# A gate in pairs of slices, fewer copies and a new instruction list in a linear-attention and expert-layer kernel

## The chip, the core and the metric

One core of a Trainium2 chip runs the whole program. The metric is device time in microseconds; for the kernel before it is the median of three runs. One further execution was taken by the hardware profiler, and all rows here are of that one.

## The reference, cut to what matters

```python
k_n = k / (norm(k) + 1e-6)
for t in range(S):                        # B, H, S, D = 4, 8, 768, 48
    y[t] = q[t] @ state
    state += beta[t] * outer(k_n[t], v[t] - k_n[t] @ state)
x = y as [3072 tokens, 384]
h = x @ w_in                              # w_in 384 x 2048
x = (h * clip(h + 3, 0, 6) / 6) @ w_out   # the dense layer, w_out 2048 x 384
# then eight experts (384 -> 1024 -> 384), each token to the one with the largest gate
```

## The kernel before

The program has two parts. The first part, which the change edits, works through the sequence in 12 chunks of 64 steps (32 rows of 4 batches times 8 heads, handled as two halves of 128 partitions, so 24 iterations `it`), and runs the first seven 128-wide slices of the dense layer's hidden width (NF1 = 7) for each chunk's 256 tokens as soon as these are known. The second part does the remaining nine slices on 512 tokens at a time, and then the experts.

The first part is written as some 30 Python generators (streams), each of which yields one engine instruction or a group. `drive` asks them in the order of the letters of ORDER, so ORDER alone sets the order in which instructions reach each engine; each engine then works its own queue in that order and waits where data are missing.

Names that recur. `kr`, `kn`, `Kbd` are the keys as loaded, normed, and split in two half-precision parts. `pG` is the product of keys with themselves, whose diagonal 32 x 32 blocks ScalarE copies to `Dt` (four copies an iteration, one for each 32 partitions); VectorE transposes `Dt` into `Bt` and solves a triangular system in `Xp` with `sub` as its scratch tile. `uH`/`uL`, `W`, `S`, `Spr` belong to the recurrence over chunks. `vsq`, `sums`, `tot`, `ptot`, `ssq`, `eiv`, `elv`, `sgv`, `sd` belong to a running sum of squares of v, from which each chunk's power-of-two scale is made: one round for each chunk. `xTH`/`xTL` are a chunk's transposed output in two parts.

`narrow_first` prepares a dense-layer weight: ScalarE takes the absolute value into `nws`, VectorE bounds it from below, and three more VectorE instructions move bits. It runs 14 times, twice for each of the seven slices.

The gate of the dense layer is in `m_stream`: for each slice nine matmuls into `ph`, 256 columns, then

```python
yield ACT.activation(t_, ph, ACTF.Relu, bias=half, scale=1.0 / 6.0)
yield DVE.scalar_tensor_tensor(t_, t_, 1.0, ph, ALU.min, ALU.mult)
yield ACT.activation(gH, t_, ACTF.Copy)
yield POOL.tensor_tensor(gL, t_, gH.bitcast(FP32), ALU.subtract)
```

and, one slice later, six matmuls of `gH`/`gL` with the second weight into `py`. `ph` has two halves of one bank used in turn, `t` one buffer of 256 columns, `gH` and `gL` two each.

In the rows nearly all of the first part has line L36, the helper that issues each instruction; the tiles tell them apart.

Of the kernel before, what the change touches and what calls it, by code (L numbers as in the profile page):

```python
# [71 lines left out]
def kernel(ctx: ExitStack, tc: tile.TileContext, q, k, v, beta, w_in, w_out, w_gate, w1, w2, out):  # L72
# [141 lines left out]
    with ExitStack() as ax:  # L214
# [136 lines left out]
        def scale_stream():  # L351

            last = None
            for s in range(NS):
                yield "next"
                yield from need(("V", s))
                sums = tmp([128, 2], FP32, "sums", 2)
                for bp in range(2):
                    yield ACT.activation(tmp([128, H, D], FP32, "vsq"), vrs[s][:, bp], ACTF.Square, accum_out=sums[:, bp:bp + 1])
                tot = tmp([128, 1], FP32, "tot", 2)  # L360
                if s:
                    yield DVE.scalar_tensor_tensor(tot, sums[:, 0:1], last, sums[:, 1:2], ALU.add, ALU.add)
                else:
                    yield DVE.tensor_tensor(tot, sums[:, 0:1], sums[:, 1:2], ALU.add)
# [10 lines left out]
                sgt[s] = dict(r=sd[:, 0:1], p=sd[:, 1:2], v=sg[:, 0], i=sg[:, 1])  # L375
                done.add(("sc", s))
# [24 lines left out]
        def n_stream():  # L401

            for g in range(NI // 4):
                yield "next"
                ss = tmp([128, 4, H], FP32, "ss")
                for j in range(4):
                    yield from need(("kl", 2 * g + j // 2))
                    sq_ = tmp([128, H, D], FP32, "ksq" if g or j % 2 else "vsq")
                    yield ACT.activation(sq_, ks[2 * g + j // 2][:, j % 2], ACTF.Square)
                    yield DVE.tensor_reduce(ss[:, j], sq_, AX.X, ALU.add)  # L410
# [418 lines left out]
        def narrow_first(src, n):  # L829
# [7 lines left out]
            yield DVE.tensor_scalar(bf, bf, 2.0 ** -15, None, ALU.max)  # L837
# [59 lines left out]
        nph = [0]  # L897
        yps = {}

        def m_stream():  # L900
            for s in range(NS):
# [3 lines left out]
                py = [clk.tile(psA, [128, 512], FP32, f"py{t}", 1, f"py{t}") for t in range(2)]  # L905
                pend = []
                for f in range(NF1 + SKM):
                    if f < NF1:
                        if not s:
                            yield from need(("wi", f))  # L910
                        fs = slice(f * 128, (f + 1) * 128)
                        ph = phb[:, nph[0] % 2]
                        nph[0] += 1
                        for c in range(KD):
                            yield [PE.matmul(ph, wi[a][:, c, fs], xt[x][:, c], start=c == 0 and n == 0, stop=c == KD - 1 and n == 2)
                                   for n, (a, x) in enumerate(((0, 0), (0, 1), (1, 0)))]
                        t_ = tmp([128, 256], FP32, "t", 1)
                        yield ACT.activation(t_, ph, ACTF.Relu, bias=half, scale=1.0 / 6.0)
                        yield DVE.scalar_tensor_tensor(t_, t_, 1.0, ph, ALU.min, ALU.mult)
                        gH, gL = tmp([128, 256], FP32R, "gH", SKM + 1), tmp([128, 256], FP32R, "gL", SKM + 1)  # L920
                        yield ACT.activation(gH, t_, ACTF.Copy)
                        yield POOL.tensor_tensor(gL, t_, gH.bitcast(FP32), ALU.subtract)
                        pend.append((f, gH, gL))
                    if f == NF1 - 1:
                        done.add(("Y", s))
                    if f >= SKM:
                        fp, gh, gl = pend.pop(0)
                        if not s:
                            yield from need(("wo", fp))
                        for t in range(2):  # L930
                            ts_ = slice(t * 128, (t + 1) * 128)
                            o = py[t][:, 0:YW]
                            yield [PE.matmul(o, gh[:, ts_], wo[0][:, fp], start=fp == 0, stop=False),
                                   PE.matmul(o, gh[:, ts_], wo[1][:, fp], start=False, stop=False),
                                   PE.matmul(o, gl[:, ts_], wo[0][:, fp], start=False, stop=fp == NF1 - 1)]
# [13 lines left out]
        def drive(streams):  # L949
# [33 lines left out]
            "kkkkkaaaakbrbbbbbsbrbbprbrpbsrbsjjrjbsrbbsqbjsnqrnqsnssqqqqqqsprnqnqnrqq1smrnronsr1mnprqrrsomsmnossn",  # L983
            "snnrssoqsmnnmmnsmsmmsrsqnrrnmosrnro0nsm0jqmmaarammmmmsqomqrsbjjsqbqrasmbmmbqmksommsmmsmkkmbrkms6rorm",
            "bmkkkmdmkmhrhssssshblrlslblqlespbrbrssslrklbrllelblblblbsblleplqsldslrlrlelnrnlnnnnllrllslelnlnnsnsl",
            "lrescslsnlqlsrrnlnllelnkllaslqessamllnrmqsrlrlmslrbmlrlmslscrnmlslmlqbnelenramsmasrqbsqscllbmlbllbll",
            "qlnsbllmmrbirnmkmmbibk7riqmsbemefmbsmserscqmqefsiifmii2sb3i3imsbs33ii2mm7misqmmibs116smfr220hf10h1h0",
            "1f0fesl11b0esnf0ls1ll0slll230ele4ln1e23n02dfni4nrq10ilf0lfinl0dililsin1isis0nirfgslg1e5li12fge5lecse",
            "al0lge0fsgnlsl0glm33tfa0lt1tltmqldnc11tts1l00ststt0t1ntelltlltmt0tllpn0pllqlqltetttnl1tmmmtfnttltml1",
            "4bl4qntttlbltmtqs1tm0nl1lltnbtsdttltttnm7qlllmstmfsqlc1mtl1lql8af8lmtntlt0ttttleq1tfltasmnmt0clfm1ll",  # L990
            "tmmmllelttttt0s1t0itttimeg50beq1ittqtbgmqb5gbmgqtgbbgbib3q22mbmmmqit7itit2tbmtqbt3ebitpp2titt080qtth",
            "ihfth0feb00ttlit0tt6tqtltlqil0itqn3f3nnllq0l2qltfld9t21llttldi4it1lini4l1tlqiqlttt0tn1tl3tc1t3ftl12e",
# [498 lines left out]
```

## Time and profile before

| | us |
|---|---|
| median of three runs (980.76 to 981.46) | 980.83 |
| profiled execution | 983.78 |
| its span, first to last instruction | 982.1 |
| TensorE busy in the span | 887.7 |
| VectorE | 584.1 |
| ScalarE | 571.4 |
| GpSimd | 429.9 |

The rows name engines as PE (TensorE), PEld (its weight loads), DVE (VectorE), ACT (ScalarE), POOL (GpSimd), SP (the queue that issues most DMAs). A group's row tells what is written from what, partitions by elements, the count, busy time, the mean of one in ns, and the idle time just before. TensorE's rows are pipelined, so that its busy time holds the tails of matmuls that overlap.

### The profile page before, as it was taken

The numbers are of one execution on the slowest core, as the hardware profiler recorded it, in microseconds if no ns is written. First come the engines' busy times: TensorE is split into PE (matmuls) and PEld (weight loads), VectorE is DVE, ScalarE is ACT, GpSimd is POOL, SyncE is SP. The second block draws the span as 40 slices with busy tenths as digits, with TensorE's granted clock in tenths as the row PEclk, the third lists the DMA queues.
The fourth block names the chain that finished last, engine by engine and source line by source line (L and its number), as shares of the span: only waits on it lengthen the run. The fifth ranks groups of instructions, "written<-read, shape, count | busy, mean of one in ns | idle before, by whom it ended". The sixth has DMA issues, their size and how long they took to land.

```text
span 982.1 us, 27912 instructions
## 1 busy us (share of the span) xinstructions
PE 887.7 (90%) x11582; PEld 822.5 (84%) x11582; DVE 584.1 (59%) x1612; ACT 571.4 (58%) x1201; POOL 429.9 (44%) x445
## 2 busy tenths in 40 slices
PE   2426999999989999999999999999999999999997
PEld 2425889889978888888788899899899999999996
DVE  8998998988879887564576455653553222121221
ACT  6858997897878967765556332333325453354521
POOL 5346555554535623333532113303105934765751
PEclk9999798999999999999989999999999999999999
DMA  7889998899697877356465233322208634533500
GB/s 148 149 159 151 170 178 150 157 158 167 149 165 149 176 168 172 92 160 218 142 200 162 99 105 116 107 65 98 91 29 289 219 98 131 176 119 116 174 21 21
DMA packets 250921, 137.85 MB, mean 140 GB/s; under 512 B 195427, under 2 KB 235685, under 8 KB 250784
## 3 DMA queue, kind: packets, MB, share of 16 engines
q1 hardware_dynamic: 242960, 117.77, 53.1%
q0 software_dynamic: 7280, 17.41, 5.4%
q8 instruction: 92, 1.51, 0.6%
q10 hardware_dynamic: 544, 0.80, 0.2%
q14 instruction: 45, 0.37, 0.1%
HBM read 71.56 MB, written 35.50 MB: 109 GB/s over the span
## 4 chain that ended last, share of the span: by engine, by line
PE 63%; DVE 18%; ACT 7%; issue 7%; POOL 3%; DMA 1%; SPq 0%; POOLq 0%; ACTq 0%; DVEq 0%
PE ph L1320 11%; PE ph L1111 9%; PE ph L36 6%; PE py L36 6%; PE py L1336 4%; PE py L1335 4%; PE py L1334 4%; PE pz L1099 3%; PE pz L1101 3%; PE pz L1100 3%; DVE Xp L36 3%; DVE sub L36 3%; PE pO L36 2%; DVE nws L36 2%; PE pW L36 2%
## 5 line engine op out<-in xcount | busy, mean ns | idle before, releaser
L1115 DVE SCALAR_TENSOR_TENSOR hL<-ph,hH 128x384 fp32r<-128x384 f32 (+6 forms) x64 | 36.1, 564 | 163.5 <-ACT hH L1114 163.5
L36 POOL TENSOR_TENSOR gL<-t,gH 128x256 fp32r<-128x256 f32 x84 | 64.8, 771 | 153.3 <-ACT gH L36 139.4
L1114 ACT ACTIVATE hH<-ph 128x384 fp32r<-128x384 f32 (+6 forms) x64 | 31.7, 495 | 105.1 <-PE ph L1111 105.1
L36 PE MATMUL ph<-xTH,wiH 128*128 128x256 f32 x252 | 76.4, 303 | 10.4 <-DVE t L36 9.5
L1323 ACT ACTIVATE t<-ph,half 128x512 f32<-128x512 f32 x54 | 37.2, 689 | 77.2 <-PE ph L1320 76.9
L1280 POOL DMA_INDIRECT slots<-row,di x24 | 23.9, 998 | 125.0 <-DVE di L1272 119.5
L1324 DVE SCALAR_TENSOR_TENSOR t<-t,ph 128x512 f32<-128x512 f32 x54 | 37.1, 687 | 65.6 <-ACT t L1323 65.4
L1099 PE MATMUL pz<-a2H,hH 128*128 128x384 f32 (+1 forms) x216 | 73.2, 339 | 0.4 <-ACT hH L1114 0.4
L1100 PE MATMUL pz<-a2L,hH 128*128 128x384 f32 (+1 forms) x216 | 72.4, 335 | 0.0
L1101 PE MATMUL pz<-a2H,hL 128*128 128x384 f32 (+1 forms) x216 | 72.4, 335 | 0.0
L1132 POOL DMA_INDIRECT out_dram<-yo,rw x29 | 28.1, 969 | 100.6 <-ACT yo L1131 96.3
L36 PE MATMUL ph<-xTL,wiH 128*128 128x256 f32 x252 | 71.1, 282 | 0.0
L36 PE MATMUL ph<-xTH,wiL 128*128 128x256 f32 x252 | 71.0, 282 | 0.0
L1328 DVE TENSOR_TENSOR gL<-t,gH 128x512 fp32r<-128x512 f32 x54 | 46.7, 865 | 32.7 <-ACT gH L1327 32.5
L36 DVE TENSOR_TENSOR Xp<-Xp,sub 128x31 f32<-128x31 f32 (+15 forms) x186 | 64.0, 344 | 2.6
L36 PE MATMUL py<-woH,gH 128*128 128x392 f32 x168 | 64.6, 384 | 0.4 <-ACT gH L36 0.4
L36 DVE TENSOR_TENSOR sub<-Bt,Xp 128x31 f32<-128x31 f32 (+15 forms) x186 | 61.7, 332 | 2.5
L36 PEld LDWEIGHTS ph<-xTH,wiH 128*128 128x128 f32 x252 | 48.0, 190 | 17.6 <-DVE t L36 15.9
L152 POOL TENSOR_TENSOR a2L<-r,a2H 128x384 fp32r<-128x384 f32 x64 | 62.6, 1008 | 0.0
L36 ACT ACTIVATE t<-ph,half 128x256 f32<-128x256 f32 x84 | 39.7, 472 | 38.0 <-PE ph L36 32.1
L152 POOL TENSOR_TENSOR a1L<-r,a1H 128x512 fp32r<-128x512 f32 x48 | 60.4, 1303 | 0.1
L36 PE MATMUL py<-woH,gL 128*128 128x392 f32 x168 | 58.5, 348 | 1.8 <-issue 1.5
(322 smaller groups left out, 3142.5 us busy)
## 6 DMA issues: line engine op xcount, KB each, us to landing
r<-in_moe_w_dram SPq DMA_DIRECT2D x32, 768.0 KB, 4.6
slots<-zrow SPq DMA_DIRECT2D x8, 784.0 KB, 6.7
stage<-in_moe_w_in_dram SPq DMA_DIRECT2D x16, 384.0 KB, 4.1
stage<-in_moe_w_out_dram SPq DMA_DIRECT2D x16, 384.0 KB, 3.6
row<-ypart SPq DMA_DIRECT2D x6, 784.0 KB, 4.4
ysave<-row SPq DMA_DIRECT2D x6, 784.0 KB, 3.6
rw<-slots SPq DMA_DIRECT2D x24, 196.0 KB, 3.0
kr<-in_k_dram SPq DMA_DIRECT2D x24, 192.0 KB, 4.8
```

Of the source, the lines that this page charges most:

```text
L36: return self.fn(*self.a, **self.k)
L152: in_order(pool.tensor_tensor(dst[1], src_ap, dst[0].bitcast(FP32), ALU.subtract))
L1099: pe.matmul(o, hh[:, ts_], a2[0][:, fp], start=fp == 0, stop=False)
L1100: pe.matmul(o, hh[:, ts_], a2[1][:, fp], start=False, stop=False)
L1101: pe.matmul(o, hl[:, ts_], a2[0][:, fp], start=False, stop=fp == KF2 - 1)
L1111: pe.matmul(ph, a1[a][:, c, fs], xt[x][:, c, 0:n], start=k == 0, stop=k == 3 * KD - 1)
L1320: pe.matmul(ph, wi(a, f)[:, c], xt[x][:, c], start=n == 0, stop=n == 3 * KD - 1)
L1323: act.activation(t_, ph, ACTF.Relu, bias=half, scale=1.0 / 6.0)
L1328: dve.tensor_tensor(gL, t_, gH.bitcast(FP32), ALU.subtract)
L1334: pe.matmul(o, gh[:, ts_], wo(0, fp), start=fp == 0, stop=False)
L1335: pe.matmul(o, gh[:, ts_], wo(1, fp), start=False, stop=False)
L1336: pe.matmul(o, gl[:, ts_], wo(0, fp), start=False, stop=fp == NF2 - 1)
```

## The change

Five things, all in the first part. The gate works on pairs of slices: `ph` is the whole bank of 512 columns, `t`, `gH`, `gL` are one buffer of 512 columns each, the seven slices become three pairs and a single, and the pair before is multiplied with the second weight between VectorE's part of the gate and the split of `t`. The running scale is made for two chunks at once from four sums of squares. The lower bound of the weights goes from VectorE to GpSimd. The diagonal blocks are copied by three instructions, the first on all 128 partitions. ORDER is another list. Besides, the squares of v go to a half-precision scratch tile, and the first squares of k use the tile `t`.

```diff
-            for s in range(NS):
-                yield "next"
-                yield from need(("V", s))
-                sums = tmp([128, 2], FP32, "sums", 2)
-                for bp in range(2):
-                    yield ACT.activation(tmp([128, H, D], FP32, "vsq"), vrs[s][:, bp], ACTF.Square, accum_out=sums[:, bp:bp + 1])
-                tot = tmp([128, 1], FP32, "tot", 2)
+            for s in range(0, NS, 2):
+                yield "next"
+                sums = tmp([128, 4], FP32, "sums", 2)
+                for n in range(4):
+                    yield from need(("V", s + n // 2))
+                    yield ACT.activation(tmp([128, H, D], FP16, "vsq"), vrs[s + n // 2][:, n % 2], ACTF.Square, accum_out=sums[:, n:n + 1])
+                tot = tmp([128, 1], FP32, "tot", 3)
+                yield DVE.tensor_reduce(tot, sums, AX.X, ALU.add)
                 if s:
-                    yield DVE.scalar_tensor_tensor(tot, sums[:, 0:1], last, sums[:, 1:2], ALU.add, ALU.add)
-                else:
-                    yield DVE.tensor_tensor(tot, sums[:, 0:1], sums[:, 1:2], ALU.add)
+                    tot_ = tot
+                    tot = tmp([128, 1], FP32, "tot", 3)
+                    yield DVE.tensor_tensor(tot, tot_, last, ALU.add)
...
-                for x in range(4):
-                    r = slice(32 * x, 32 * x + 32)
-                    c = slice(32 * (x % 2), 32 * (x % 2) + 32)
+                for r, c in ((slice(0, 128), slice(0, 32)), (slice(32, 64), slice(32, 64)), (slice(96, 128), slice(32, 64))):
                     yield ACT.activation(Dt[r, :, 8 * j:8 * j + 8], p_[r, :, c].rearrange("p u i -> p i u"), ACTF.Copy)
...
-            yield DVE.tensor_scalar(bf, bf, 2.0 ** -15, None, ALU.max)
+            yield POOL.tensor_scalar(bf, bf, 2.0 ** -15, None, ALU.max)
...
+                for fp in pairs + [None]:
+                    if fp is not None:
+                        w = len(fp) * 256
+                        ph = phb.rearrange("p x t -> p (x t)")[:, 0:w]
+                        for n_, f in enumerate(fp):
+                            if not s:
+                                yield from need(("wi", f))
+                            fs = slice(f * 128, (f + 1) * 128)
+                            for c in range(KD):
+                                yield [PE.matmul(phb[:, n_], wi[a][:, c, fs], xt[x][:, c], start=c == 0 and n == 0, stop=c == KD - 1 and n == 2)
+                                       for n, (a, x) in enumerate(((0, 0), (0, 1), (1, 0)))]
+                        t_ = tmp([128, 512], FP32, "t", 1)[:, 0:w]
                         yield ACT.activation(t_, ph, ACTF.Relu, bias=half, scale=1.0 / 6.0)
                         yield DVE.scalar_tensor_tensor(t_, t_, 1.0, ph, ALU.min, ALU.mult)
...
+                    if pend:
+                        fq, gh, gl = pend.pop(0)
+                        for n_, f in enumerate(fq):
...
+                    if fp is not None:
+                        gH, gL = [tmp([128, 512], FP32R, x, 1)[:, 0:w] for x in ("gH", "gL")]
                         yield ACT.activation(gH, t_, ACTF.Copy)
                         yield POOL.tensor_tensor(gL, t_, gH.bitcast(FP32), ALU.subtract)
...
         ORDER = [
-            "kkkkkaaaakbrbbbbbsbrbbprbrpbsrbsjjrjbsrbbsqbjsnqrnqsnssqqqqqqsprnqnqnrqq1smrnronsr1mnprqrrsomsmnossn",
+            "kkkkkaabbbjjaasbkbbbjbojobobobsbbsprpbpbbsnssnrrnqrnrprsnsssosnoqqmoorsqnmqnorrnnqmqnsrssqrqqmqnmrnm",
```

On VectorE, near the start of the program, from the first norm of k to the first bits of the weights, before:

```order
L36 TENSOR_SCALAR nws<-nws 128x384
L36 TENSOR_SCALAR s_177<-s_177 128x32
L36 TENSOR_SCALAR nws<-nws 128x384
L36 RECIPROCAL s_182<-s_177 128x32
L36 SCALAR_TENSOR_TENSOR nws<-stage,nws 128x384
L36 TENSOR_TENSOR s_182<-s_182,ss 128x32
L36 TENSOR_SCALAR nws<-nws 128x384
L36 SCALAR_TENSOR_TENSOR nws<-stage,nws 128x384
L36 TENSOR_TENSOR s_182<-s_182,s_177 128x32
L36 TENSOR_SCALAR nws<-nws 128x384
L36 TENSOR_SCALAR s_182<-s_182 128x32 x2
```

and of the change, at the same place:

```order
L36 TENSOR_SCALAR s_179<-s_179 128x32
L36 COPY bT<-pb 128x12x8
L36 RECIPROCAL s_188<-s_179 128x32
L36 TENSOR_TENSOR s_188<-s_188,ss 128x32
L36 TENSOR_TENSOR s_188<-s_188,s_179 128x32
L36 TENSOR_SCALAR s_188<-s_188 128x32 x2
L36 RECIPROCAL rn<-s_188 128x32
L36 TENSOR_SCALAR nws<-nws 128x384
L36 TENSOR_TENSOR kn<-kr,rn 128x384
L36 SCALAR_TENSOR_TENSOR nws<-stage,nws 128x384 x2
```

The norm of k is no longer mixed with the weights' rows, and of each weight's two one-input rows (TENSOR_SCALAR nws) one is gone from VectorE.

On ScalarE, the last 256 tokens of the first part, from the first slices' `t` on, before (`wt`, `nw`, `wo0H`, `wi0H` prepare weights of the second part):

```order
L36 ACTIVATE t<-ph,half 128x256
L36 ACTIVATE wt<-pwt 128x384
L36 ACTIVATE gH<-t 128x256
L36 ACTIVATE wo0H<-wc 128x8
L36 ACTIVATE t<-ph,half 128x256
L36 ACTIVATE gH<-t 128x256
L36 ACTIVATE nw<-stage 128x384
L36 ACTIVATE t<-ph,half 128x256
L36 ACTIVATE gH<-t 128x256
```

and of the change:

```order
L36 ACTIVATE t<-ph,half 128x512
L36 ACTIVATE gH<-t 128x512
L36 ACTIVATE wo0H<-wc 128x8
L36 ACTIVATE t<-ph,half 128x512
L36 ACTIVATE nw<-stage 128x384
L36 ACTIVATE gH<-t 128x512
L36 ACTIVATE wi0H<-nw 128x3x128
L36 ACTIVATE t<-ph,half 128x512
```

Three `t` rows of 512 columns stand where six of 256 stood; the order of `t`, `gH` and the next `t` is the same.

On ScalarE, ahead of the last group's diagonal copies and behind the first of them, before:

```order
L36 ACTIVATE t<-ph,half 128x256
L36 ACTIVATE Dt<-pG 32x32x8 x3
L36 ACTIVATE gH<-t 128x256
L36 ACTIVATE Dt<-pG 32x32x8
L36 ACTIVATE MC_113<-pG 128x256
```

and of the change:

```order
L36 ACTIVATE Dt<-pG 128x32x8
L36 ACTIVATE xr<-pO,qsc_6921 128x384
L36 ACTIVATE Dt<-pG 32x32x8 x2
L36 ACTIVATE t<-ph,half 128x512
L36 ACTIVATE Spr00H<-S_127,sgv_8230 128x384
L36 ACTIVATE Spr10H<-S_128,sgv_8230 128x384
L36 ACTIVATE gH<-t 128x512
L36 ACTIVATE MC_113<-pG 128x256
```

Four `Dt` rows became three, and two rows of the recurrence (`Spr`) stand between a pair's `t` and its `gH`.

## Rows read from the trace of the kernel before

**Rows 1.** VectorE's instructions on the tile xTL: count, ns min/median/max, first and last start.

```profile
L36 DVE TENSOR_TENSOR xTL<-pX,xTH x24: 482/550/558, 107.8 to 463.5; 128x384 fp32r<-128x384 f32 x24
```

**Rows 2.** Three stages: busy us of each engine (instructions), granted clock, DMA.

```profile
0.00:112.60 112.60, 51.70 (x1220) 46.99 (x1222) 102.73 (x307) 83.64 (x178) 57.68 (x62) 0.96 0.89 154
112.60:464.00 351.40, 330.35 (x7538) 309.62 (x7533) 279.98 (x832) 278.27 (x606) 164.14 (x166) 0.98 0.81 161
464.00:487.00 23.00, 20.14 (x127) 16.53 (x126) 13.85 (x40) 12.99 (x30) 10.04 (x18) 1.00 0.42 135
```

**Rows 3.** Chain of work in the three stages: shares by line, single pieces (start, us).

```profile
by line: DVE nws L36 16.8%; DVE Xp L36 9.3%; DVE sub L36 8.6%; issue 6.4%; DVE W L36 6.0%; DMA kr<-in_k_dram 4.7%; DVE Bt L36 4.1%; DVE ss L36 3.4%; POOL TT L36 2.8%; DVE Kbd L36 2.5%; SPq L36 2.0%; DVE uL L36 1.9%; DVE s L36 1.8%; ACT TT L
...
by line: PE ph L36 15.9%; PE py L36 15.4%; issue 7.2%; PE pO L36 6.6%; DVE Xp L36 5.8%; DVE sub L36 5.6%; PE pW L36 5.1%; DVE t L36 2.9%; PE pZ L36 2.7%; PE pP L36 2.4%; ACT t L36 2.3%; ACT Dt L36 1.8%; ACT W L36 1.7%; DVE uL L36 1.7%; PE p
...
406.94 2.34 PE py L36 x12
...
469.73 1.29 PE ph L36 x9
```

**Rows 4.** Timeline of ScalarE in stage C: start, us, instruction, [idle before <-releaser].

```profile
468.74 0.47 ACT L36 ACTIVATE t<-ph,half 128x256 f32<-128x256 f32 x1
...
481.65 0.47 ACT L36 ACTIVATE t<-ph,half 128x256 f32<-128x256 f32 x1 [0.54 <-POOL gL L36]
```

**Rows 5.** VectorE's groups by form, 0 to 487 us: count | busy us, mean ns | idle.

```profile
L36 DVE SCALAR_TENSOR_TENSOR t<-t,ph 128x256 f32<-128x256 f32 x84 | 34.9, 416 | 39.9 <-ACT t L36 39.2
...
L36 DVE TENSOR_SCALAR nws<-nws 128x384 f32<-128x384 f32 x14 | 7.9, 564 | 0.2 <-ACT nws L36 0.2
...
L36 DVE SCALAR_TENSOR_TENSOR tot<-sums,tot 128x1 f32<-128x1 f32 x11 | 5.5, 502 | 0.0
...
L36 DVE TENSOR_SCALAR sd<-sgv 128x1 f32<-128x1 f32 x24 | 3.3, 146 | 0.1
```

**Rows 6.** VectorE's instructions on the tile nws, 0 to 480 us: ns min/median/max.

```profile
L36 DVE TENSOR_SCALAR nws<-nws x28: 318/354/2019, 10.6 to 110.7; 128x384 f32<-128x384 f32 x14, 128x384 int32<-128x384 int32 x14
```

**Rows 7.** GpSimd's groups by form, 0 to 487 us.

```profile
L36 POOL TENSOR_TENSOR gL<-t,gH 128x256 fp32r<-128x256 f32 x84 | 64.8, 771 | 153.3 <-ACT gH L36 139.4 <-issue 8.6 <-PE pR L36 2.5
...
L36 POOL TENSOR_TENSOR kn<-kr,rn 128x384 f32<-128x384 f32 x20 | 16.6, 830 | 8.7 <-DVE rn L36 8.0
...
L36 POOL TENSOR_TENSOR woL<-nws,woH 128x384 fp32r<-128x384 f32 x7 | 7.8, 1111 | 16.1 <-ACT woH L36 16.1
...
L136 POOL MEMSET zrow<- 128x392 f32 x1 | 0.4, 426 | 0.0
```

**Rows 8.** ScalarE's groups by form, 0 to 487 us.

```profile
L36 ACT ACTIVATE t<-ph,half 128x256 f32<-128x256 f32 x84 | 39.7, 472 | 38.0 <-PE ph L36 32.1 <-POOL gL L36 5.0 <-PE pX L36 0.4
L36 ACT ACTIVATE Dt<-pG 32x256 f32<-32x256 f32 x96 | 35.8, 373 | 6.3 <-PE pG L36 5.0
L36 ACT ACTIVATE gH<-t 128x256 fp32r<-128x256 f32 x84 | 34.7, 413 | 13.9 <-DVE t L36 12.6
...
L36 ACT ACTIVATE MC<-pG 128x256 f16<-128x256 f32 x24 | 9.2, 382 | 0.3
```

**Rows 9.** Groups by form of the second part, 490 to 740 us, where slices are 512 columns.

```profile
L1323 ACT ACTIVATE t<-ph,half 128x512 f32<-128x512 f32 x54 | 37.2, 689 | 77.2 <-PE ph L1320 76.9
L1324 DVE SCALAR_TENSOR_TENSOR t<-t,ph 128x512 f32<-128x512 f32 x54 | 37.1, 687 | 65.6 <-ACT t L1323 65.4
L1327 ACT ACTIVATE gH<-t 128x512 fp32r<-128x512 f32 x54 | 34.1, 631 | 36.0 <-DVE t L1324 36.0
```

**Rows 10.** GpSimd's group of the page on 512 columns.

```profile
L152 POOL TENSOR_TENSOR a1L<-r,a1H 128x512 fp32r<-128x512 f32 x48 | 60.4, 1303 | 0.1
```

**Rows 11.** Waits, 112.6 to 464 us: total us, times, longest us.

```profile
PEld ph L36 <- DVE t L36: 12.6, 16, 1.7
```

**Rows 12.** Windows of 2 us around a fall of the granted clock (PEclk).

```profile
146.00:148.00 2.00, 0.43 (x2) 0.43 (x3) 1.82 (x6) 1.93 (x4) 0.00 (x0) 0.72 1.23 251
148.00:150.00 2.00, 2.00 (x30) 1.91 (x30) 0.67 (x1) 0.55 (x3) 1.72 (x2) 0.50 1.42 186
```

More of the change, by code (lines that the diff above doesn't have):

```diff
@@ L374, in scale_stream @@
                 yield DVE.tensor_scalar(sd[:, 1:2], sg[:, 1], D12, None, ALU.mult)
-                sgt[s] = dict(r=sd[:, 0:1], p=sd[:, 1:2], v=sg[:, 0], i=sg[:, 1])
-                done.add(("sc", s))
+                for n in range(2):
+                    sgt[s + n] = dict(r=sd[:, 0:1], p=sd[:, 1:2], v=sg[:, 0], i=sg[:, 1])
+                    done.add(("sc", s + n))
         def bd_rows(dst, src, eng=POOL):
@@ L407, in n_stream @@
                     yield from need(("kl", 2 * g + j // 2))
-                    sq_ = tmp([128, H, D], FP32, "ksq" if g or j % 2 else "vsq")
+                    sq_ = tmp([128, H, D], FP32, "ksq") if g or j % 2 else tmp([128, 512], FP32, "t")[:, 0:DM].rearrange("p (u d) -> p u d", d=D)
                     yield ACT.activation(sq_, ks[2 * g + j // 2][:, j % 2], ACTF.Square)
@@ L905, in m_stream @@
                 py = [clk.tile(psA, [128, 512], FP32, f"py{t}", 1, f"py{t}") for t in range(2)]
+                pairs = [range(f, min(f + 2, NF1)) for f in range(0, NF1, 2)]
                 pend = []
[L907 to L917, printed above, removed]
+                for fp in pairs + [None]:
[10 more added lines that the diff above has]
+                        t_ = tmp([128, 512], FP32, "t", 1)[:, 0:w]
@@ L918, in m_stream @@
                         yield ACT.activation(t_, ph, ACTF.Relu, bias=half, scale=1.0 / 6.0)
                         yield DVE.scalar_tensor_tensor(t_, t_, 1.0, ph, ALU.min, ALU.mult)
-                        gH, gL = tmp([128, 256], FP32R, "gH", SKM + 1), tmp([128, 256], FP32R, "gL", SKM + 1)
+                        if fp[-1] == NF1 - 1:
+                            done.add(("Y", s))
+                    if pend:
+                        fq, gh, gl = pend.pop(0)
+                        for n_, f in enumerate(fq):
+                            if not s:
+                                yield from need(("wo", f))
+                            for t in range(2):
+                                ts_ = slice(n_ * 256 + t * 128, n_ * 256 + (t + 1) * 128)
+                                o = py[t][:, 0:YW]
+                                yield [PE.matmul(o, gh[:, ts_], wo[0][:, f], start=f == 0, stop=False),
+                                       PE.matmul(o, gh[:, ts_], wo[1][:, f], start=False, stop=False),
+                                       PE.matmul(o, gl[:, ts_], wo[0][:, f], start=False, stop=f == NF1 - 1)]
@@ L921, in m_stream @@
+                    if fp is not None:
+                        gH, gL = [tmp([128, 512], FP32R, x, 1)[:, 0:w] for x in ("gH", "gL")]
                         yield ACT.activation(gH, t_, ACTF.Copy)
                         yield POOL.tensor_tensor(gL, t_, gH.bitcast(FP32), ALU.subtract)
[L923 to L935, printed above, removed]
+                        pend.append((fp, gH, gL))
@@ L988 @@
[L988 to L992, printed above, removed]
@@ L1014 @@
+            "dtftit100ttdut1ttuuuttt21u2utuu4u98utu40tttt2tt3u1tttgg55gf3ug1u0ggutteu1ttfttttttt1ftfu0tu0ft3tuutu",
+            "tutt8tuu8t01fututttutt0tf0u1ttt10ttutu8uttuutututttttttt4t1141ttuuttftu1tgt5gt5ggg9uuutgtttttutttttt",
+            "uttttutttututuuttutututututututttttttuttuttttuuutuu9uttttutttuttuttuttu8898",
         ]
```

50 lines of the change are left out of this document (24 added, 26 removed).

## The prediction

> **What bounds the kernel now.** The change edits only the part ahead of 487 us, where the second program part begins. I read that part in three stages, cut where the first 256 tokens are transposed (the xTL rows, two for each 256 tokens, run from 107.8 to 463.5 us [rows 1]; the second ends at 112.6) and where the last are.
>
> Stage A, 0 to 112.6 us: VectorE is busy 102.7 of 112.6 us, ScalarE 83.6, GpSimd 57.7, TensorE 51.7 [rows 2]. The chain of work is a chain of VectorE rows: the weights' bit moves (nws) 16.8%, the triangular solve (Xp, sub) 17.9%, the other VectorE lines behind them [rows 3]. Here VectorE's own sum sets the time. The load of k at the chain's start, 4.7% or 5.3 us [rows 3], is touched by nothing here.
>
> Stage B, 112.6 to 464 us: three engines are near full, TensorE 330 of 351 us, VectorE 280, ScalarE 278 [rows 2]. The chain changes engines all the time: PE ph and py 31%, pO 6.6%, the solve 11.4%, and, of what is edited, DVE t 2.9%, ACT t 2.3%, ACT Dt 1.8% [rows 3]. So no single sum sets the time, and what an edit is worth is bounded by what it has on the chain.
>
> Stage C, 464 to 487 us: the seven slices of the last 256 tokens with almost nothing beside them. TensorE is busy 20.1 of 23 us [rows 2], but each slice's ScalarE row starts 2.58 us after the one before it (468.74 to 481.65 in five steps [rows 4]), while nine ph matmuls take 1.29 us and twelve py matmuls 2.34 us, six of them 1.17 [rows 3]: 2.46 us at most, less as the pieces include a pipeline's tail. The chain from ph over ScalarE, VectorE and GpSimd back to ScalarE (the wait of 0.54 us for gL [rows 4]) sets the beat.
>
> **The change, part by part.**
>
> Bound on GpSimd: 14 VectorE rows of 564 ns go [rows 5], 7.9 us, all of them in stage A (the VectorE rows nws of this kind and its neighbour run from 10.6 to 110.7 us [rows 6]). The GpSimd row that comes in place has no row of before. Below it lies a GpSimd write alone of 392 columns, 426 ns; above it a two-input GpSimd row of the same 384 columns in the same stage, 1111 ns; kn, two inputs without conversion, takes 830 [rows 7]. I take 750 ns, nearer to kn, as it reads one input: 14 x 0.75 = 10.5 us (6.0 to 15.6). GpSimd goes from 57.7 to 68 of 112.6 us, so the sum does not bind; the hop adds some 0.2 to 0.5 us to each weight's chain, which the other weight's chain covers. The rows of these VectorE instructions run from 318 to 2019 ns [rows 6]: an instruction that can take 318 was held for up to 1.7 us. What holds it isn't named; GpSimd being at work is one reading. The Trainium skill (page "SBUF — State Buffer", section on the two separate sides) says that GpSimd and a VectorE instruction in a two-port mode share one port pair as an exclusive lock for a whole instruction; the long rows agree with it, and by it the move cuts both ways, since it takes 14 candidates from VectorE and gives GpSimd 14 holders. By the rows alone VectorE saves 7.9; with the price of the rival below, it loses 2.6.
>
> Scale for two chunks: of 12 rounds 6 go. A round is one tot row (502 ns) and nine one-column rows like sd (146 ns) [rows 5]: 1.8 us, and a new round has a reduction and, five times of six, an addition, some 0.3 us, in place of tot. 12 x 1.8 - 6 x 1.6 = 12 us by rows. Short VectorE rows overlap: the 92 groups of the view of [rows 5] add up to 457 us, count by mean, against 396.6 us of busy time in the three stages [rows 2], so I count 0.87 of it, 10 us, of which 2 rounds lie in stage A (2.5 us). The work is hidden among other work in stage B; were VectorE alone the bound, it would be worth 7.5 there.
>
> Gate in pairs, per 256 tokens: seven slices become three pairs and one single. ScalarE t: 7 x 472 = 3304 ns become 3 x 689 + 472 = 2539, so 0.77 us, 9.2 in 12 chunks. VectorE t: 7 x 416 become 3 x 687 + 416, 0.44 us, 5.2 in all. ScalarE gH: 7 x 413 become 3 x 631 + 413, 0.59 us, 7.0 in all [rows 5, 8, 9]. GpSimd gL: 771 against 1303 for 512 columns (a1L): 12 x (5.4 - 4.7) = 8.6 us less [rows 7, 10], which about pays for the bounds. TensorE's matmuls keep their count and shape. The hand-overs fall from 84 to 48.
>
> Three diagonal copies: 24 of 96 Dt rows of 373 ns go [rows 8], the wide one reads all 128 partitions at the same 256 columns; the row of MC with that shape is within 3% of it in the same view, so I add nothing: 9.0 us of ScalarE.
>
> The list: every engine's order is new. On TensorE the mix is the same as before: at each sixth transposition as many slices' ph matmuls stand ahead of it as before, and of py within two. So I take the list as one of like quality, and give it no term, but width.
>
> **Sum.** Stage A: VectorE loses 7.9 + 2.5 = 10.4 us by its rows. VectorE is 91% busy there; I count 8 (0, if the move is paid back by waits, to 11). Stage B: on the chain, ScalarE t falls by 23% of 2.3%, VectorE t by 15% of 2.9%, Dt by a quarter of 1.8%, of 351 us: 1.9 + 1.5 + 1.6 = 5 us. TensorE's weight loads stood 12.6 us behind a VectorE t, 16 times [rows 11]; 33 of 77 hand-overs go, so 43% of it, 5 us, of which I count 4. Together 9 (0 to 16; the upper end is ScalarE's whole relief in stage B, 0.85 of 25 us, less a quarter that its idle time hides). Stage C: TensorE's work is 7 x 2.2 = 15.4 us plus about 1 for the two weights' products. Exposed stay the first pair's ScalarE and VectorE rows, 0.69 + 0.69 + about 0.4 of hops, 1.8, then the single's tail, some 1.5: 19.7 against 23, so 3 (0 to 5). In a pair the chain t, t, gH, gL is 0.69 + 0.69 + 0.63 + 1.30 + 0.4 = 3.7 us against 4.4 of matmuls: it no longer sets the beat.
>
> 8 + 9 + 3 = 20 us. The profiled execution took 983.8 us (span 982.1 and 1.7 around it), so 963.8; the median of the runs is 980.8, 3 less, and on that scale I forecast **961 us**, with 953 to 967 as the likeliest case's own range.
>
> **Clock.** TensorE's granted clock falls to half in four places. The one at 148 us follows 1.6 us in which TensorE had next to no work (0.43 us busy of 2, then clock 0.50 [rows 12]). A new order has its own gaps; one such stretch of 6 us in which TensorE is the bound costs 3. I let it widen the range by 3 to either side.
>
> **Rivals.**
>
> 1. Stage B does not move: TensorE is 94% busy there and its work is unchanged, so what is taken from ScalarE and VectorE only becomes idle time. For it: 31% of the chain is ph and py. Against it: busy counts pipelined tails, and 12.6 us of waits for t stand in the rows. Then 8 + 3 = 11 us: 970.
>
> 2. GpSimd holds VectorE: each of the 14 bounds keeps a VectorE row waiting for its 0.75 us, so 10.5 us are given back in stage A, and 9.5 us of gain stay: 971. For it are the rows up to 2019 ns. Against it: 14 VectorE rows that could be held are gone. It is the way in which the time would come out by the rule of the Trainium skill cited above.
>
> 3. One buffer ties ScalarE to TensorE (slower). gH and gL had two buffers of 256 columns, and have one of 512. A pair's gH can't be written before TensorE has done the pair's predecessor, 12 py matmuls, 2.34 us. If it arrives half a block early, ScalarE stands for 1.17 us at each of the 44 pairs and singles up to stage C, 51 us, with uH, Spr and W of the recurrence queued behind it; ScalarE has 73 idle us in stage B (351 - 278) that take some. With half on the path, 26 us, net 6 slower: 987. It decides from 0.9 us per pair on. Against it: in the new list 0 to 11 ScalarE rows stand between a pair's t and its gH, 3.7 on the mean against 1.6 before, which is time for the matmuls.
>
> 4. The relief goes through fully: stage A 11, stage B 16, stage C 5, with better packing on the chain: 980.8 - 32 = 949.
>
> **Chances.** The forecast 0.50, rival 1 0.17, rival 2 0.07, rival 4 0.09, rival 3 0.17, of which 0.06 ends within 2 us of no change (0.2%, about what a measurement of this kernel can tell from none) and 0.11 above. So faster 0.83, same 0.06, slower 0.11. The range from 949 to 978 holds the forecast, rivals 1 and 2, half of rival 4 and a little of rival 3, and reaches over the clock's 3 us.
>
> **What the next profile would show.** Stage A right: the last nws rows of VectorE and the first xTL about 8 us earlier, GpSimd rows nws at 0.43 to 1.1 us, no more VectorE rows over 1 us than before. Gate right: 36 ScalarE t rows near 689 ns, TensorE waits for t below 8 us, in stage C a pair every 4.2 to 4.6 us. Rival 3: idle time of ScalarE ahead of gH put down to TensorE py, which has no row now. Dt right: 24 rows of 128 partitions near 380 ns; at 500 they give back a third of the 9 us. The forecast is wrong above all if stage B's length, 351 us, does not change or grows: then the new list or the buffers took what the shorter rows gave.

## The result, and the profile after

The changed kernel takes **969.77 us** (median of four runs, 968.33 to 970.05) beside 981.14 of the kernel before (four runs, 980.76 to 982.27): ratio **0.9874**, 95% interval 0.9855 to 0.9892. Faster by 11.4 us, where 20 were forecast. The profiled execution took 969.57 us, its span is 967.8 against 982.1. The same three windows as in [rows 2], cut at the same events (end of the second xTL row, end of the last, first ph of the second part); behind the stage come the busy us of PE, PEld, DVE, ACT and POOL, the granted clock and the DMA share:

```profile
0.00:117.70 117.70, 48.84 (x1153) 43.92 (x1153) 99.87 (x269) 78.00 (x166) 71.17 (x73) 0.97 0.77 144
117.70:451.30 333.60, 322.19 (x7588) 306.00 (x7588) 281.28 (x768) 265.38 (x530) 160.47 (x136) 0.99 0.85 172
451.30:474.80 23.50, 19.14 (x120) 17.98 (x120) 14.09 (x37) 10.51 (x23) 8.63 (x15) 0.93 0.35 118
```

Stage A grew from 112.6 to 117.7 (forecast: 8 less), stage B fell from 351.4 to 333.6 (forecast: 9 less), stage C went from 23.0 to 23.5 (forecast: 3 less), and the second part, untouched, from 495.1 to 493.0. So the sum hides two errors of opposite sign.

**Stage A.** The tile nws, instructions of the whole span (ns min/median/max, first to last start), against [rows 6], and VectorE's groups by form and its waits in 0 to 117.7 us:

```profile
L36 POOL TENSOR_SCALAR nws<-nws x14: 1159/1166/1484, 11.6 to 120.7; 128x384 f32<-128x384 f32 x14
L36 DVE TENSOR_SCALAR nws<-nws x14: 296/360/2096, 13.3 to 123.4; 128x384 int32<-128x384 int32 x14
```

```profile
L36 DVE TENSOR_SCALAR nws<-nws 128x384 int32<-128x384 int32 x13 | 7.2, 552 | 4.9 <-POOL nws L36 4.9
...
L36 DVE COPY W<-TT 32x512 f16<-32x512 f16 x8 | 3.9, 505 | 0.0
...
L36 DVE TENSOR_TENSOR kn<-kr,rn 128x384 f32<-128x384 f32 x4 | 3.0, 757 | 0.1
L36 DVE TENSOR_SCALAR s<-s 128x32 f32<-128x32 f32 x9 | 2.8, 312 | 0.4 <-ACT s L36 0.3
```

```profile
DVE nws L36 <- POOL nws L36: 4.9, 5, 2.4
DVE MC L36 <- ACT MC L36: 3.9, 3, 2.9
```

The bound costs GpSimd 1.17 us at the median, not 0.75. VectorE lost the bound's 7.9 us of rows, but its other rows grew: in stage A of before these four groups had means of 384, 276, 554 and 175 ns, so 2.2 + 1.8 + 0.8 + 1.2 = 6.0 us came back. The copies' 1.8 us of it are one hold, which runs with the bound on VectorE show as well (below). VectorE's busy time fell by 2.9 us only, its idle time rose from 9.9 to 17.8. Two waits name 7.6 of these 7.9 us: 4.9 for the bound, new, and 2.7 more for MC, 1.2 us before and 3.9 after, one of them 2.9 long: the new list puts MC there in VectorE's queue, and the wait stays at 4.2 us where e1 takes the bound back.

How a row grows is seen in the timelines of GpSimd and of VectorE near 36 us (start, us):

```profile
34.56 1.48 POOL L36 TENSOR_SCALAR nws<-nws 128x384 f32<-128x384 f32 x1 [0.53 <-ACT nws L36]
36.02 0.20 POOL L36 TENSOR_TENSOR woL<-wc,woH 128x8 fp32r<-128x8 f32 x1
36.16 1.80 POOL L36 MEMSET W<- 128x2048 f16 x1
```

```profile
36.08 2.10 DVE L36 TENSOR_SCALAR nws<-nws 128x384 int32<-128x384 int32 x1 [0.48 <-POOL nws L36]
...
43.91 0.36 DVE L36 TENSOR_SCALAR nws<-nws 128x384 int32<-128x384 int32 x1 [2.36 <-POOL nws L36]
```

The same instruction takes 0.36 us where GpSimd stands still and 2.10 where GpSimd works on other tiles: it ends at 38.18, just behind GpSimd's row (37.96). The Trainium skill (page "SBUF — State Buffer", section on the two separate sides) says that of the two engines on the shared port pair the loser is blocked for the other's whole instruction; this pair of rows agrees. The held row is the one that the bound releases: it can start when the bound ends, at 36.04, which is when GpSimd goes on to its next rows. Beside a bound itself little is held. I estimate from the timelines, taking each VectorE row against the lower quartile of its form in four profiles, that in all of stage A the rows beside a bound ran over by 1.2 us, those beside GpSimd's other rows by 8.0, against 6.8 before (rows over by less than 0.06 us left out).

A second case had a consequence, but it isn't the bound's. Two copies of VectorE for W took 2.31 us in the change, while GpSimd worked from 105.39 to 107.40 on Kbd and Pst. Here are the same two copies in VectorE's timelines of the change, of e9 (the bound on VectorE) and of e5 (the change's own instructions up to here), then windows of 2 us of the change around them, with the columns of the first fence:

```profile
105.25 2.31 DVE L36 COPY W<-TT 32x512 f16<-32x512 f16 x2
...
101.75 2.34 DVE L36 COPY W<-TT 32x512 f16<-32x512 f16 x2
...
103.81 0.49 DVE L36 COPY W<-TT 32x512 f16<-32x512 f16 x2
```

```profile
104.00:106.00 2.00, 1.67 (x80) 1.59 (x77) 1.97 (x8) 1.98 (x5) 0.61 (x1) 1.00 0.94 181
106.00:108.00 2.00, 0.00 (x0) 0.00 (x0) 1.97 (x2) 0.23 (x1) 1.41 (x2) 0.54 0.41 151
108.00:110.00 2.00, 1.74 (x55) 1.69 (x55) 2.00 (x8) 1.67 (x3) 0.00 (x0) 0.50 0.02 8
110.00:112.00 2.00, 2.00 (x45) 1.89 (x43) 1.94 (x6) 1.93 (x6) 1.70 (x2) 0.50 0.04 8
```

TensorE had nothing for 2 us (its pO waited 2.6 us for VectorE's S), and its granted clock then stood at half (1.2 GHz) until about 113 us. Whether this hold comes is a matter of some 0.1 us: GpSimd's row Kbd starts 0.14 us behind the first copy here, 0.17 in e9, and 0.27 in e5, where the copies aren't held. The new list has the hold with the bound on GpSimd (the change, e4, e10) and on VectorE (e8, e9), and lacks it with either (e5, e6, e7; e1). e4 and e5 issue the change's instructions in its order through stage A: with the hold it lasts 117.7 and 117.8 us, without it 114.2. So some 3.5 of the 5.1 us come with the hold, whichever engine does the bound. The kernel before has half clock there too (102.5 to 112.8 us).

**Stage B.** The gate's groups by form over the span, against [rows 5, 7, 8], and waits in 117.7 to 451.3 us, against [rows 11]:

```profile
L36 POOL TENSOR_TENSOR gL<-t,gH 128x512 fp32r<-128x512 f32 x36 | 47.7, 1325 | 73.5 <-ACT gH L36 70.0 <-PE pW L36 3.2
...
L36 ACT ACTIVATE t<-ph,half 128x512 f32<-128x512 f32 x36 | 24.6, 684 | 23.0 <-PE ph L36 22.9
L36 DVE SCALAR_TENSOR_TENSOR t<-t,ph 128x512 f32<-128x512 f32 x36 | 24.6, 683 | 19.1 <-ACT t L36 18.7
...
L36 ACT ACTIVATE gH<-t 128x512 fp32r<-128x512 f32 x36 | 22.6, 629 | 11.4 <-PE py L36 7.2 <-DVE t L36 3.8
```

```profile
ACT gH L36 <- PE py L36: 9.3, 13, 1.6
...
PEld ph L36 <- DVE t L36: 0.6, 2, 0.4
```

All four durations are within 2% of the forecast. TensorE's wait for t, 12.6 us before, is 0.6. Rival 3's wait, which had no row, now has one: ScalarE's gH for TensorE's py, 9.3 us in 13 places.

Not all of the 17.8 us need be the gate's. TensorE's granted clock stood at half for 13.6 us of this stage before, in three stretches, and for 3.4 us after, in one (windows on these stretches, three of before, then one of the change):

```profile
146.90:153.70 6.80, 6.13 (x83) 5.94 (x84) 3.52 (x8) 4.22 (x10) 3.07 (x2) 0.50 1.39 188
222.00:225.40 3.40, 3.40 (x18) 3.40 (x15) 2.21 (x6) 1.13 (x3) 1.14 (x1) 0.50 0.97 295
280.00:283.40 3.40, 3.40 (x47) 2.95 (x48) 0.00 (x0) 2.31 (x5) 0.00 (x0) 0.50 1.06 304
...
321.20:324.60 3.40, 3.40 (x17) 3.40 (x18) 1.37 (x7) 1.60 (x4) 0.66 (x1) 0.50 0.93 129
```

TensorE was busy through nearly all of it, so an estimate by half of these lengths is up to 5 us of the 17.8. The longest stretch began in a wait for t (1.62 us, up to 147.57); ahead of the other two stood gaps of other tiles (pO, pG). That they vanish in the change isn't explained.

**Stage C.** VectorE's timeline, then the one long wait in TensorE's, then windows of 1 us:

```profile
463.14 0.69 DVE L36 SCALAR_TENSOR_TENSOR t<-t,ph 128x512 f32<-128x512 f32 x1 [1.17 <-ACT t L36]
463.75 1.17 DVE L36 TENSOR_SCALAR nw<-nw 128x384 f32<-128x384 f32 x4
464.84 3.03 DVE L36 SCALAR_TENSOR_TENSOR nw<-stage,nw 128x384 int32<-128x384 int32 x4
467.79 1.46 DVE L36 TENSOR_SCALAR nw<-nw 128x384 f32<-128x384 f32 x2
469.28 1.15 DVE L36 SCALAR_TENSOR_TENSOR nw<-stage,nw 128x384 int32<-128x384 int32 x2
470.35 0.41 DVE L36 SCALAR_TENSOR_TENSOR t<-t,ph 128x256 f32<-128x256 f32 x1
```

```profile
467.54 0.52 PE L36 MATMUL pwt<-ident,nw 128*128 128x128 f32 x3 [2.68 <-DVE nw L36]
```

```profile
465.00:466.00 1.00, 0.00 (x0) 0.00 (x0) 1.00 (x2) 0.00 (x0) 0.97 (x1) 1.00 0.00 0
466.00:467.00 1.00, 0.00 (x0) 0.00 (x0) 1.00 (x2) 0.00 (x0) 0.51 (x1) 1.00 0.00 0
...
468.00:469.00 1.00, 1.00 (x6) 1.00 (x5) 0.97 (x2) 0.24 (x1) 0.97 (x1) 0.50 0.23 42
469.00:470.00 1.00, 1.00 (x4) 1.00 (x4) 0.93 (x3) 1.00 (x3) 0.03 (x1) 0.50 0.67 184
```

Between pair 3's t and the single's t VectorE does 12 rows nw for weights of the second part. A transposition of these weights stands in TensorE's queue ahead of the single's last ph matmuls, so TensorE stands for 2.68 us and then works at half clock: its py matmuls start 0.33 us apart (468.46, 468.79), later 0.18 (471.40, 471.58).

### The profile page after: what moved, and what is told of

The parts are those of the page before. It is cut to its first block, busy times and chain, and to the rows that moved or that the text cites. A ratio compares the mean times of both kernels' runs of the same rounds, so it can differ in the third digit from the quotient of the medians.

```text
span 967.8 us, 27606 instructions
## 1 busy us (share of the span) xinstructions
PE 872.6 (90%) x11570; PEld 814.5 (84%) x11570; DVE 581.7 (60%) x1507; ACT 550.2 (57%) x1105; POOL 438.6 (45%) x423
## 4 chain that ended last, share of the span: by engine, by line
PE 71%; DVE 13%; issue 6%; POOL 4%; ACT 4%; DMA 1%; SPq 0%; POOLq 0%; ACTq 0%
PE ph L1320 11%; PE ph L1111 9%; PE py L36 8%; PE ph L36 7%; PE py L1335 4%; PE py L1336 4%; PE py L1334 4%; PE pz L1099 3%; PE pz L1101 3%; PE pz L1100 3%; PE pO L36 3%; PE pW L36 3%; DVE Xp L36 2%; DVE sub L36 2%; DVE nw L36 2%
## 5 line engine op out<-in xcount | busy, mean ns | idle before, releaser
L36 POOL TENSOR_TENSOR gL<-t,gH 128x512 fp32r<-128x512 f32 (+1 forms) x48 | 56.9, 1186 | 108.1 <-ACT gH L36 95.9
L36 PE MATMUL py<-woH,gH 128*128 128x392 f32 x168 | 61.3, 365 | 0.0
L1111 PE MATMUL ph<-yTL,a1H 128*128 128x384 f32 (+5 forms) x168 | 58.3, 347 | 0.0
L1111 PE MATMUL ph<-yTH,a1L 128*128 128x384 f32 (+5 forms) x168 | 58.3, 347 | 0.0
L1111 PE MATMUL ph<-yTH,a1H 128*128 128x384 f32 (+5 forms) x168 | 58.2, 346 | 0.0
```

Source lines behind the costliest of these rows:

```text
L36: return self.fn(*self.a, **self.k)
L1111: pe.matmul(ph, a1[a][:, c, fs], xt[x][:, c, 0:n], start=k == 0, stop=k == 3 * KD - 1)
```

## The experiments

The theories. **G**: the bound on GpSimd costs stage A its gain. **L**: the new list is the worse one there. **P** against **W** for stage B: fewer hand-overs, or shorter sums of rows. How far a stage of one profile can be read: e9 below has e1's instructions in e1's order through stages A and B, and its stages differ from e1's by 1.8 and 4.1 us, the end of B by 2.3; e4 and e5 have the change's instructions through stage A, and end it at 117.8 and 114.2 us; e4 has them through stage B too, which takes 336.0 against 333.6. So a stage's change below some 4 us is no evidence by itself, and totals are compared by their ratios to the kernel before (1% is 9.8 us).

**e1_bound_dve.** The change, with the bound back on VectorE.

```diff
-            yield POOL.tensor_scalar(bf, bf, 2.0 ** -15, None, ALU.max)
+            yield DVE.tensor_scalar(bf, bf, 2.0 ** -15, None, ALU.max)
```

> The changed kernel with the weights' bound back on VectorE, nothing else. Theory G (the GpSimd bounds, 1.2 us each in a weight's chain and holding VectorE rows, made the first stage 5 us longer): the second xTL ends 6 to 12 us earlier than its 117.7 us, and the time falls from 969.8 to 958 to 965, since the later stages hold TensorE 97% busy whenever they start. Theory L (the new list made the first stage longer, whichever engine does the bound): the second xTL ends at 117 us or later, by up to the 7.9 us that VectorE gets back, and the time is 969 to 977.

Measured: 965.77 us (965.19 to 966.80), ratio 0.9839 (0.9821 to 0.9857). Windows of its stages, then its stage A groups of VectorE:

```profile
0.00:112.80 112.80, 49.60 (x1153) 44.70 (x1153) 98.93 (x282) 78.52 (x166) 55.32 (x60) 1.00 0.81 151
112.80:448.00 335.20, 323.35 (x7588) 307.35 (x7588) 281.54 (x769) 265.56 (x530) 159.23 (x135) 0.99 0.85 171
```

```profile
L36 DVE TENSOR_SCALAR nws<-nws 128x384 f32<-128x384 f32 x13 | 6.0, 460 | 0.6 <-ACT nws L36 0.5
...
L36 DVE TENSOR_SCALAR nws<-nws 128x384 int32<-128x384 int32 x13 | 5.1, 392 | 0.1
```

VectorE is busy for *less* time with 13 more rows (98.9 against 99.9), the int32 row is back at 392 ns, and stage A ends 4.9 us earlier. Part of this is the hold of the copies, which this profile doesn't have. Like with like it is less: with the hold 117.7 (the change) against 114.5 (e9, the bound on VectorE), without it 114.2 (e5) against 112.8, so 1.4 to 3.2 us, which stages alone can't prove. The whole falls by 3.4 us by the ratios, whose intervals just touch; no run of e1 is as slow as the fastest of the change. This speaks for G, with less than it expected (965.77 beside 958 to 965). It also shows what G leaves over: without the bound's move stage A is as long as before, though two scale rounds are gone.

**e2_bound_pool_old.** The kernel before, with only the bound moved to GpSimd: the opposite edit.

> The kernel before with the bound on GpSimd, alone, with the old list. Theory G: the second xTL ends at 119 to 125 us instead of 112.6, and the time rises from 981 to 987 to 993. Theory L: the VectorE rows that go pay for the GpSimd rows, the second xTL ends within 2 us of 112.6, time 979 to 983.

Measured: 996.75 us (993.03 to 998.86), ratio 1.0139 (1.0112 to 1.0166); stage A 123.8 us, 11.2 longer. The tile nws, and two groups of VectorE in stage A:

```profile
L36 POOL TENSOR_SCALAR nws<-nws x14: 1157/1164/1345, 10.9 to 119.6; 128x384 f32<-128x384 f32 x14
```

```profile
L36 DVE TENSOR_SCALAR nws<-nws 128x384 int32<-128x384 int32 x14 | 9.1, 650 | 4.4 <-POOL nws L36 4.1
...
L36 DVE TENSOR_SCALAR s<-s 128x32 f32<-128x32 f32 x9 | 5.1, 570 | 0.4 <-ACT s L36 0.3
```

Alone, the edit makes the kernel slower, more so than the 987 to 993 us expected. G holds with either list, and the new list bears the move better (3.4 us in place of 13.6 by the ratios), so L as the only cause of a longer stage A falls. Here too the large holds stand beside GpSimd's other rows, not the bounds: by the same estimate 16.5 us against 2.9.

**e3_no_bound.** The change without the bound at all (this part of the computation is left out).

```diff
-            yield POOL.tensor_scalar(bf, bf, 2.0 ** -15, None, ALU.max)
+            yield []
```

> The changed kernel without the lower bound of the weights at all (that part of the computation is left out): a floor for what the bound costs anywhere. Theory G: second xTL 8 to 14 us earlier than 117.7, time 955 to 962, and at most 5 us below the kernel with the bound on VectorE. Theory L: second xTL at 113 us or later, time 965 or more.

Measured: 961.50 us (960.22 to 963.58), ratio 0.9796 (0.9773 to 0.9818), stage A 109.7 us (a profile without the hold). The bound is worth 7.7 us by the ratios on GpSimd and 4.2 on VectorE. Even a bound that costs nothing takes stage A only 2.9 us below the kernel before, not 8.

**e4_tail.** The change, with the last letters of the list in another order, so that the second part's weights come behind the gate.

```diff
-ututut tttttt u tt u tttt uuu t uu 9 u tttt u ttt u tt u tt u tt u 8898
+ututut tttttt u tt ttt ttt tt uuuuuu 9 tttt tt tt tt uuuuuu 8898
```

(blanks are set here for reading; u is the second part's weights, t the gate, 9 the result's transfer)

> The changed kernel with the last 45 letters of the list in another order: the single slice's gate ahead of the last weight's preparation, and that weight's two TensorE steps behind the last matmuls of the gate. If the 2.7 us in which TensorE waits for VectorE's nw rows in the last stage, and the half clock behind it, cost what they seem to, the last stage falls from 23.5 to 19 to 21 us and the time to 966 to 968. The rival: the weight's preparation is only late elsewhere, the second part's first block waits for it, and the time stays at 969 to 971 though the last stage is shorter.

Measured: 974.83 us (971.50 to 978.52), ratio 0.9924 (0.9901 to 0.9948); stage C 27.1 us. A failure, by the edit's own fault: the transfer that frees yp went out late, and a wait between 453 and 481 us names it.

```profile
ACT yp L36 <- DMA ypart<-yp: 4.0, 1, 4.0
```

It tells nothing of the theory; e9 repeats it better.

**e5_narrow.** The change, with the gate's wide rows cut in two at the same places of the list.

```diff
-                        yield ACT.activation(t_, ph, ACTF.Relu, bias=half, scale=1.0 / 6.0)
+                        hv = [slice(x, x + 256) for x in range(0, w, 256)]
+                        yield [ACT.activation(t_[:, x], ph[:, x], ACTF.Relu, bias=half, scale=1.0 / 6.0) for x in hv]
```

and so for VectorE's t, gH and gL.

> After the change, with the gate's four instructions of 512 columns each issued as two of 256, one right behind the other, at the same places of the order. Blocks stay pairs and the one buffer stays, so TensorE hands over as often as after the change. It tells the two halves of the gate's term apart. Theory P (the hand-over in pairs is what stage B gained, since the waits of TensorE for t vanished): little comes back, stage B 334 to 339 us against 333.6, and the whole 970 to 976. Theory W (the wider rows, some 30 us less of ScalarE, VectorE and GpSimd, are what it gained): most of the 17.9 us come back, stage B 343 us or more, the whole 979 or more.

Measured: 974.61 us (972.37 to 979.45), ratio 0.9924 (0.9900 to 0.9947), 4.9 us worse than the change by the ratios; stage B 339.7. Nearer to P: 6 of stage B's 17.8 us come back (3.7 against e4's 336.0). VectorE starts on no pair before ScalarE has done both halves, so the hand-overs are those of the change. The waits of TensorE for t stay small:

```profile
PEld ph L36 <- DVE t L36: 2.0, 5, 0.5
```

**e6_dt4.** The change, with four diagonal copies of 32 partitions again.

```diff
-                for r, c in ((slice(0, 128), slice(0, 32)), (slice(32, 64), slice(32, 64)), (slice(96, 128), slice(32, 64))):
...
+                for xs in ((0, 1), (2,), (3,)):
```

> After the change, with four diagonal copies of 32 partitions again (two of them at one place of the order). ScalarE gets 24 rows of some 375 ns more, 9 us. If the prediction's bookkeeping by the share of the chain holds (a quarter of 1.8% of stage B), 1.6 to 2.5 us come back: 971 to 972.5. If ScalarE's load is what sets stage B, the 9 us come back in the most part: 976 or more. If the wider idle time of ScalarE hides them: within 1 us of 969.8.

Measured: 971.71 us (970.35 to 973.04), ratio 0.9890 (0.9869 to 0.9912): 1.6 us worse by the ratios, the size that the share of the chain gave, though the intervals overlap. ScalarE's 9 us are not worth 9.

**e7_scale2.** The change, with each one-column VectorE row of a scale round issued twice (nine more rows a round, into scratch tiles).

> After the change, with the one-column VectorE instructions of each scale round issued a second time into a scratch tile: the load of six more rounds (some 9 us of VectorE by rows), without more rounds in the order. Theory S (VectorE sets stage A, in stage B this work is hidden): stage A 1 to 3 us longer, stage B within 2, the whole 971 to 974. If VectorE's load sets stage B too, the whole is 976 or more.

Measured: 971.33 us (968.55 to 972.09), ratio 0.9877 (0.9855 to 0.9899): not to be told from the change. A cost of 2 us would be within the intervals, and the time lies in theory S's range too, so whether the rows of the scale are hidden in stage A stays open (116.6 us here, 114.2 in e5, both without the hold). That VectorE's load sets stage B as well, 976 or more, falls.

**e8_list.** e1 with the edits of e5, e6 and e7 as well: of the change only the list and the blocks of two slices stay.

> What is left when all four shortenings are undone and only the list and the blocks of two slices stay: the bound on VectorE, four diagonal copies, gate rows of 256 columns, doubled scale rows. Theory P (the pairs' hand-overs and the list that goes with them gain most of stage B): still faster than before, stage A about 114, stage B about 341 us, the whole 972 to 977. Theory W: back at the time before, 980 to 985, or slower.

Measured: 975.12 us (973.66 to 980.13), ratio 0.9934 (0.9913 to 0.9955). Windows of stages A and B, and TensorE's wait in stage B:

```profile
0.00:115.90 115.90, 48.47 (x1153) 43.50 (x1153) 101.22 (x291) 81.20 (x174) 55.10 (x60) 0.93 0.80 147
115.90:454.50 338.60, 323.48 (x7588) 305.81 (x7588) 286.31 (x848) 279.78 (x612) 164.88 (x168) 1.00 0.84 169
```

```profile
PEld ph L36 <- DVE t L36: 2.2, 5, 0.7
```

ScalarE has more to do in stage B than before (279.8 against 278.3), VectorE too (286.3 against 280.0), and the stage is still 12.8 us shorter. But it has no half clock, and the stage before had 13.6 us of it, up to 7 of the 12.8. By the ratios 6.5 us of e1's 15.8 stay and 9.3 go with the three shortenings. So P holds for a part, the hand-overs and the order around them, and the shorter rows for another; how large each is isn't shown. Blocks of two and the list can't be told apart here, since the blocks need a list of their own.

**e9_tail3.** e1, with the single's rows and pair 3's py ahead of the second part's weights in the last row of the list, and the transfer early.

```diff
-uttttutttututuuttutututututututttttttuttuttttuuutuu9uttttutttuttuttuttu8898
+ut9tttutttututuuttutututututututttttttuttuttttttuttttuttuttuuuttttuuuuu8898
```

> The bound on VectorE as in e1_bound_dve (965.8 us, stage C 23.3), and in the last stage the order changed at one place: the single slice's ph, t, t, gH and gL, and pair 3's py ahead of the weights' rows of the second part (three nw rows of VectorE, a transposition and its copy), with the result's transfer kept early. In e1_bound_dve VectorE's t of the single came 1.9 us after ScalarE's t started, with four nw rows ahead of it. Theory C (the second part's weight rows on VectorE stand in front of the single's t, and this is why stage C did not get shorter): stage C 21 to 22.3 us, the second part no longer, the whole 963 to 965. Rival (the weights are needed as early as they come): stage C shorter or not, the second part or the stage longer by as much, the whole 965.5 or more.

Measured: 966.88 us (965.76 to 970.67), ratio 0.9864 (0.9840 to 0.9888). Windows of stage C and of the first 6.6 us of the second part:

```profile
445.70:468.40 22.70, 17.81 (x120) 16.43 (x120) 12.96 (x37) 10.28 (x23) 8.32 (x9) 1.00 0.38 123
468.40:475.00 6.60, 6.60 (x23) 5.31 (x24) 1.68 (x7) 2.78 (x6) 5.60 (x18) 0.74 0.91 302
```

Stage C is 0.6 us shorter, at full clock, and the second part 2.8 longer: it begins with the clock at 0.74, where e1 has 1.00 in its first 6.6 us. The rival holds: the weights that were put back have to be waited for (TensorE 1.92 us at a pwc), and the stretch of half clock moved with them.

**e10_half.** The change, with the bound of the seven output weights on VectorE and that of the seven input weights on GpSimd.

```diff
-            yield POOL.tensor_scalar(bf, bf, 2.0 ** -15, None, ALU.max)
+            yield (DVE if n else POOL).tensor_scalar(bf, bf, 2.0 ** -15, None, ALU.max)
```

> After the change, with half of the bounds on VectorE: those of the 7 output weights; those of the 7 input weights stay on GpSimd. If each bound on GpSimd costs the same, half of the 4.0 us between the whole and e1_bound_dve: 967 to 968.5, and VectorE's waits for the bound in stage A fall from 4.9 us to about 2.5. If the two weights' chains cover one another when only one goes over GpSimd: 965 to 966.5, and waits under 1 us.

Measured: 968.15 us (967.75 to 969.76), ratio 0.9873 (0.9852 to 0.9894). The wait fell as one price for each bound says, below the 2.5 us expected:

```profile
DVE nws L36 <- POOL nws L36: 2.0, 3, 1.1
```

The time says less: its median lies between those of the change and e1, its ratio is that of the change. Inconclusive for the total.

## Why the prediction was right, and where it was wrong

**The sign, the time within the range, and the rows** were right: every duration of the gate, and the diagonal copies (379 and 376 ns). That the time came within the range is in part luck: stage A missed by 13 us and stage B made up for 9 of them. The measured time lies outside the likeliest case's 953 to 967, at the 970 and 971 of rivals 1 and 2, neither of which describes the whole of what happened.

**The step that failed is stage A's**: "VectorE loses 7.9 + 2.5 = 10.4 us by its rows. VectorE is 91% busy there; I count 8 (0, if the move is paid back by waits, to 11)". It came out at +5.1, some 3.5 of which come with the hold of the copies. Three things were mis-sized. The GpSimd bound took 1166 ns at the median, above the upper bound of 1111, where I took 750 because it reads one input. The hop to GpSimd and back was said to be covered by the other weight's chain; VectorE waited 4.9 us for it. And rival 2, with 0.07, was right that GpSimd holds VectorE, but not in its price: beside the bounds themselves rows ran over by some 1.2 us, not 10.5; the large holds stand beside GpSimd's other rows, one of them met by the row that a bound releases. e1 gives 3.4 us back by the ratios, e2 shows 13.6 for the same edit with the old list. The rows up to 2019 ns [rows 6] were the evidence: the longest, at 28.02 us before, stands beside a memset of GpSimd from 28.03. I weighed it by counting rows that would be gone, in place of asking what GpSimd does next. I had also put 0 as the worst case: a row moved can cost more than it weighs.

The scale's 2.5 us in stage A did not arrive: e1, without the move, has a stage A as long as before. e7 puts the rows back, and its total shows no effect that can be measured. In its place stands a wait of the list, VectorE's MC for ScalarE (1.2 us before, 3.9 after, 4.2 in e1), and a list "of like quality" was wrong here. That this wait takes just the scale's gain was not tried apart.

**Stage B** was right in mechanism as far as that was tried, and half its size: 9 forecast, 17.8 measured (15.4 with e4's). The term "43% of it, 5 us, of which I count 4" took only the hand-overs that vanish; the wait vanished nearly whole, 0.6 us. That those that stay have work ahead of them in the list is my reading and wasn't tried apart. Up to 5 us more are half clock that went, for which the sum had no term. By the totals the shorter rows weigh more than the sum has for them: 4.9 us go when only the gate's are cut (e5; 3.4 in the sum), 9.3 when all three kinds are undone (e8). Rival 4's 16 us for this stage was the better number; rival 1 falls.

**Stage C** missed its 3 us. The sum took the second part's weights for their products on TensorE alone ("about 1 for the two weights' products"), and left their rows on VectorE out: TensorE stood 2.68 us behind their rows on VectorE, and then had some 3.5 us at half clock, which is 1.7 lost. e9 shows that moving them back does not pay either.

**Rival 3** exists as a wait, 9.3 us, but at 0.2 us for each of 44 blocks it stays far below the 0.9 from which it decides. A second buffer was not tried.

**The best version** is e1_bound_dve, 965.77 us: 1.6% faster than the kernel before, and ahead of the change (its slowest run, 966.80, is below the change's fastest, 968.33).

## What to carry to other kernels

Before a row is moved from VectorE to GpSimd, price it at the slowest GpSimd row of the same tile, and no lower for having one input. Then ask what GpSimd does when it ends, since the VectorE row that it releases can be held by that: rows whose maximum is several times their median are the sign. Where one engine's queue hands over to another in small blocks, doubling the block, here together with a new list, can take away nearly the whole wait and not only the share of hand-overs saved. Before two profiles are compared stage by stage, look for the stretches of half clock in each. And in a stage's sum, list every row that stands in the queues between the first and the last row of interest, also those that belong to the next part.

## What was unexpected of the hardware

A one-input GpSimd row (max with a constant, 128x384 f32) took 1166 ns at the median, longer than the two-input kn of the same size, 830 [rows 7], and three times VectorE's 354 [rows 6]. One VectorE row took 0.36 us alone and 2.10 beside GpSimd's memset. A single such hold, 2.31 us in two copies, left TensorE without work for 2 us, and its clock at 0.50 until 113 us; it decides some 3.5 us of stage A, and comes or stays away by about 0.1 us in when GpSimd's row starts (0.14 and 0.17 us behind the first copy with it, 0.27 without).
